# The end of the first block of a fused retention and Mish kernel: the next block's attention output one group of products sooner, its scores before the last small product, its sums before the last output addition

## The chip, the cores and the metric

The kernel runs on one core of one Trainium2 chip. The metric is the device time of one execution, in microseconds. Three runs of the kernel before took 198.63, 197.92 and 197.9 us, a median of 197.92 us. The profile is a further execution of its own.

The core's engines work side by side, each through its own list of instructions, and they meet at semaphores: TensorE (PE in the profile, with its weight loads as PEld), VectorE (DVE), ScalarE (ACT), GpSimd (POOL), and SyncE (SP), which here only issues transfers.

## The reference

The inputs are q, k and v of 4 batches, 8 heads, 768 positions and 64 features, and two weight matrices of 512 by 2048 and 2048 by 512. First comes a recurrence with a decay for each head, then a layer with the Mish activation on its 3072 rows:

```
gamma = 1.0 - 2.0 ** (-5.0 - arange(H))
for t in range(S):
    state = gamma * state + einsum('bhd,bhe->bhde', k[:, :, t], v[:, :, t])
    y[:, :, t] = einsum('bhd,bhde->bhe', q[:, :, t], state) / sqrt(D)
x = y.transpose(0, 2, 1, 3).reshape(B * S, H * D)
h = x @ w_in
g = h * tanh(log1p(exp(h)))
out = g @ w_out
```

## The kernel before, in words

The 3072 rows are cut into 24 chunks of 128 positions, six to a batch. In each chunk the recurrence becomes matrix products: scores of keys against queries, a mask (a product with a triangle), scores times values for the present chunk, the state carried from the chunks before times the queries for the past, and an outer product of keys and values for the next state. The chunks are worked in blocks: a first block of four chunks (0 to 3) and then ten blocks of two (4 and 5, 6 and 7, and so on). After the attention output of a block comes its first weight product with Mish, called g1 here, and then its second one, g2.

The blocks of two do both weight products with seven part products in place of eight, over sums and differences of quarters of the operands. Two sets of sums matter here. `x_sums` (lines 639 to 646) makes four sums of quarters of the attention output of a block, four VectorE instructions on lines 643 to 646. Inside `g1_seven`, `snap` copies a part product from PSUM to SBUF on ScalarE (line 677), and `plus` adds it to another part product on VectorE (line 687).

The order of all instructions is written out by hand: each engine does its own in the order in which the functions are called, and a semaphore makes it wait where it needs another engine's work. An engine that waits for one instruction starts nothing that stands behind it. While block n is in its second product, the attention output of block n+1 is made: `scores` (line 438), `mask` (line 444), and `y_two`, which makes the present part (line 507), the outer products (line 453) and the past part (line 489 for the first batch, 498 for others) on TensorE, and then copies the result to SBUF as `xt` on ScalarE (line 540).

The change lies in `first_g2`, the second product of the first block. Its 512 rows are four row groups, written as (p, i) with pair p and i of 0 or 1. Each row group has an output of 512 columns, which is gathered in one PSUM bank: t0[p] for (p, 0), with halves pb and pe, and t1[p] for (p, 1), with halves px and pz. The 2048 features of the hidden layer are in four slices of 512. Slices 0 and 2 go through the seven products, slices 1 and 3 through plain ones. All of first_g2's products but those of slice 3 are on line 1007. Slice 3 comes last, in `end` (line 1065): for each row group two times two matrix products of 512 columns, first half 0 for all four row groups, then half 1 for all four, and behind each half 1 the closing work `ended`: for i = 0 one VectorE addition of 512 columns (line 1071), for i = 1 a VectorE addition of 256 columns (line 1073) and a ScalarE copy of the other 256 (line 1074), which waits for that addition.

Behind first_g2, `x_sums(1)` is called, and then `g1_seven` of block 1 (chunks 4 and 5). Its PSUM tiles take the banks over as they come free: the first product (px) takes the bank of (0, 0), the second (pb) that of (0, 1), the plain product h0 that of (1, 0), and pe that of (1, 1). These are the steps of g1_seven's beginning, in its order:

```
mm(px, a(0, 0), b(0, 0), True)     # 8 matmuls, L670
m1 = snap(px)                      # ACT copy, L677
mm(pb, a(0, 1), b(1, 0), True)     # 8 matmuls, L670
c11 = plus(pb, m1)                 # DVE, L687
h0 = plain(1, 0)                   # 8 matmuls, L694
mm(px, s(2), t(2))                 # 8 matmuls, L670, adds to px
mish_of(0, 0, c11)                 # ACT, L681
u2 = snap(px)                      # ACT copy, L677
mm(pe, s(1), t(1), True)           # 8 matmuls, L670
```

The fifth product adds to the same px that m1 is copied from, so it waits until that copy is done.

Of the kernel before, what the change touches and what calls it, by code (L numbers as in the profile page):

```python
# [16 lines left out]
def kernel(  # L17
# [81 lines left out]
    for c in range(2):  # L99
        t = tri_first[c * HB:(c + 1) * HB]  # L100
# [26 lines left out]
    FIRST = 1  # L127
# [60 lines left out]
    def cast_wout(s, on_act=0):  # L188
        src = wtmps.pop(("out", s))
        t = wouts[s] = cpool.tile([P, FPS, d_model], FP16, name=f"wout{s}")  # L190
        n = FPS - on_act
        if n:
            nc.vector.tensor_copy(t[:, :n], src[:, :n])
        for f in range(n, FPS, 2):
            nc.scalar.copy(t[:, f:f + 2], src[:, f:f + 2])
# [161 lines left out]
    def room16(g):  # L357
        if g not in cast:
            qk16 = castp.tile([P, 2, H, D], FP16, name="qk16")
            cast[g] = (qk16[:, 0], qk16[:, 1], castp.tile([P, H, D], FP16, name="v16"), qk16)  # L360
        return cast[g]
# [6 lines left out]
    def cast_q(g):  # L368
        if g < NCK:
            f = qs.rearrange("p (x j) -> p x j", x=2).unsqueeze(3)  # L370
            nc.gpsimd.tensor_tensor(  # L371
                by_head(g, room16(g)[0]), by_head(0, loaded[g][0]),
                f.broadcast_to((P, 2, HP, D)), op=ALU.mult)

    def bring_k(g):
        if g < NCK:
            b, c = divmod(g, NCH)
            src = k[b, :, c * C:(c + 1) * C].rearrange("h p d -> p h d")
            if g < NCH:
                nc.gpsimd.dma_start(room16(g)[1], src)  # L380
                return
            for x in range(2):
                nc.gpsimd.dma_start(  # L383
                    room16(g)[1][:, x::2], src[:, HP * x:HP * x + HP])

    def cast_v(g):
        if g < NCK:
            nc.gpsimd.tensor_tensor(  # L388
                room16(g)[2], loaded[g][2], vs.unsqueeze(2).broadcast_to((P, H, D)), op=ALU.mult)

    def casts(g):
        cast_q(g)
        cast_v(g)

    def gate(x):
        nc.gpsimd.tensor_copy(gate_t, x)  # L396
# [45 lines left out]
    def mask(g):  # L442
        am = tpp.tile([P, 2, HP, C], FP16, name="am")
        nc.vector.tensor_tensor(  # L444
            am, ats.pop(g), tri.unsqueeze(1).unsqueeze(1).broadcast_to((P, 2, HP, C)),
            op=ALU.mult)
        ams[g] = am
# [127 lines left out]
    def some_late(n):  # L575
        for _ in range(min(n, len(late))):
            late.pop(0)()
# [57 lines left out]
    def x_part(blk, i, j):  # L635
        n = NBP // 2
        return xts[blk][:, i * n:(i + 1) * n, j * P:(j + 1) * P]

    def x_sums(blk):
        t = tsums[blk] = hp.tile([P, 4, NBP // 2, P], FP16, name="xsum", tag="xsum")  # L640
        sub = ALU.subtract
        b = [[x_part(blk, i, j) for j in range(2)] for i in range(2)]
        nc.vector.tensor_tensor(t[:, 0], b[0][1], b[0][0], op=sub)
        nc.vector.tensor_tensor(t[:, 1], b[1][1], t[:, 0], op=sub)
        nc.vector.tensor_tensor(t[:, 2], b[1][1], b[0][1], op=sub)
        nc.vector.tensor_tensor(t[:, 3], b[1][0], t[:, 1], op=sub)
# [320 lines left out]
    def g_sum(n):  # L967
        def part(s, i):
            g = gtiles[0, s // 2][:, s % 2 * FPS:(s % 2 + 1) * FPS]
            return g.rearrange("p f (a i t) -> p f a i t", a=2, i=2)[:, :, :, i]  # L970
        s1, s2, s3, s4 = [
            gsums[0].rearrange("p s (f a) t -> p s f a t", a=2)[:, i] for i in range(4)]
        if n == 1:
            nc.vector.tensor_tensor(s1, part(0, 1), part(2, 1), op=ALU.add)
        elif n == 2:
            nc.vector.tensor_tensor(s2, s1, part(0, 0), op=ALU.subtract)
        elif n == 3:
            nc.vector.tensor_tensor(s3, part(0, 0), part(0, 1), op=ALU.subtract)
        else:
            nc.vector.tensor_tensor(s4, part(2, 0), s2, op=ALU.subtract)  # L980

    def first_g2():
        hf = d_model // 2
        pairs = range(CPB // 2)
        t1 = [mmps.tile([P, 2, hf], FP32, name="o_ps", tag="mm") for _ in pairs]
        t0 = [mmps.tile([P, 2, hf], FP32, name="o_ps", tag="mm") for _ in pairs]
        osb = [[op.tile([P, 2, hf], FP32, name="osb", tag="osb") for _ in range(2)] for _ in pairs]
        m5 = [op.tile([P, hf], FP32, name="snap", tag="snap", bufs=3) for _ in pairs]
        pb, pe = [t[:, 0] for t in t0], [t[:, 1] for t in t0]
        px, pz = [t[:, 0] for t in t1], [t[:, 1] for t in t1]  # L990
        sums = gsums[0].rearrange("p s (f a) t -> p s f (a t)", a=2)

        def a(p, i, s):
            return lambda f: gts[0, s * FPS + f][:, (2 * p + i) * P:(2 * p + i + 1) * P]

        def sm(p, i):
            return lambda f: sums[:, i - 1, f, p * P:(p + 1) * P]

        def b(s, j):
            return lambda f: wouts[s][:, f, j * hf:(j + 1) * hf]  # L1000

        def t(i):
            return lambda f: tmats[(i - 1) // 2][:, (i - 1) % 2, f]

        def mm(o_ps, x, w, first=False, last=False):
            for f in range(FPS):
                nc.tensor.matmul(  # L1007
                    o_ps, x(f), w(f), start=first and f == 0, stop=last and f == FPS - 1,
                    skip_group_check=True)

        for p in pairs:
            mm(px[p], a(p, 0, 0), b(0, 0), True)
            nc.scalar.copy(osb[p][0][:, 0], px[p])
        for p in pairs:
            mm(pe[p], sm(p, 1), t(1), True)
            nc.scalar.copy(m5[p], pe[p])
        cast_wout(2, 2)
        some_late(1)
        gate(tmats[0][:, 1, 0, :1])
        casts(CPB)  # L1020
        cast_q(CPB + 1)
        some_late(1)
        g_sum(4)
        some_late(1)
        for p in pairs:
            mm(pz[p], a(p, 1, 1), b(1, 1))
        for p in pairs:
            mm(pb[p], a(p, 0, 1), b(1, 0))
        for p in pairs:
            mm(pb[p], a(p, 0, 2), b(2, 0))  # L1030
        for p in pairs:
            mm(pe[p], a(p, 0, 1), b(1, 1))
        for p in pairs:
            mm(px[p], sm(p, 2), t(2))
            nc.scalar.copy(osb[p][0][:, 1], px[p])
        turn(CPB, True)
        for p in pairs:
            mm(px[p], sm(p, 3), t(3))
            nc.vector.tensor_tensor(osb[p][1][:, 1], px[p], m5[p], op=ALU.add)
        bring_k(CPB + 2)  # L1040
        bring_k(CPB + 3)
        cast_v(CPB + 1)
        for p in pairs:
            mm(pe[p], sm(p, 4), b(2, 1))
        some_late(1)
        outer_fifth(CPB)
        turn(CPB + 1)
        decay_of_first(CPB, nc.vector)
        cast_wout(3, FPS)
        for p in pairs:  # L1050
            mm(px[p], a(p, 1, 1), b(1, 0))
        for p in pairs:
            mm(px[p], a(p, 1, 2), t(4))
        scores(CPB)
        scores(CPB + 1)
        mask(CPB)
        mask(CPB + 1)
        cast_v(CPB + 2)
        cast_q(CPB + 2)
        turn_by_dma(CPB + 2)  # L1060
        load_q(CPB + 4)

        def end(p, i, half):
            for f in range(2 * half, 2 * half + 2):
                nc.tensor.matmul(  # L1065
                    (t0, t1)[i][p], a(p, i, 3)(f), wouts[3][:, f], start=False,
                    stop=f == FPS - 1, skip_group_check=True)

        def ended(p, i):
            if i == 0:  # L1070
                nc.vector.tensor_tensor(osb[p][0], t0[p], osb[p][0], op=ALU.add)
            else:
                nc.vector.tensor_tensor(osb[p][1][:, 1], pz[p], osb[p][1][:, 1], op=ALU.add)
                nc.scalar.copy(osb[p][1][:, 0], px[p])
            row0 = (2 * p + i) * P
            stores.append((1, out[row0:row0 + P], osb[p][i].rearrange("p j c -> p (j c)")))

        ends = [(p, i) for p in pairs for i in range(2)]
        for p, i in ends:
            end(p, i, 0)  # L1080
        for p, i in ends:
            if (p, i) == (1, 0):
                y_two(1)
            end(p, i, 1)
            ended(p, i)

    def turn_and_load(g):
# [61 lines left out]
        }  # L1149

    first_block()
    x_sums(FIRST)
    gsums.append(gp.tile([P, 4, NFB // 2, P], FP16, name="gsum", tag="g0"))
    for blk in range(FIRST, len(BLOCKS)):
        steps = steps_of_first(blk) if blk == FIRST else steps_of(blk)
# [33 lines left out]
```

## Time and profile before

| | us |
|---|---|
| three runs | 198.63, 197.92, 197.9 |
| median | 197.92 |
| the profiled execution's own time | 198.56 |
| its span | 196.8 |
| PE busy | 189.7 |
| PEld busy | 157.9 |
| DVE busy | 141.8 |
| ACT busy | 105.4 |
| POOL busy | 93.1 |

The span runs from the first to the last instruction of the profiled execution; 1.76 us of its time lie outside. Times in the views below are microseconds from the start of the span. In a timeline a row gives the start, the time from the start of the first of the merged instructions to the end of the last, the engine, the line, the operation, the tiles written and read, the shape, and how many instructions were merged; brackets give idle time before it and what ended that. An instruction that needs nothing else starts before its forerunner on the engine has fully ended, so the distance from start to start is often shorter than the duration. The granted clock of TensorE is 1.00 in every stretch.

The change bears on about 42 to 55 us of the span: the end of the first block's second product and the beginning of block 1.

### The profile page before, as it was taken

The page shows a single profiled execution, that of the slowest core. Times are in us where ns is not written, and L with a number is a line of the kernel's source. Part 1 is how long each engine was busy: PE and PEld are TensorE (multiplying, and loading weights), DVE is VectorE, ACT ScalarE, POOL GpSimd, SP SyncE. Part 2 cuts the span into 40 slices and gives each one's busy share as a digit, 9 for nine tenths or more (in the row PEclk, how much of TensorE's full clock was granted, in tenths as well). Part 3 has the DMA queues.
Part 4 walks back from the last instruction along what each step waited for, and adds up shares of the span by engine and source line. Part 5 has one row for each costly group of instructions (what it writes and reads, how often), then busy time and mean ns, then how long its engine had stood idle before and what let it go on. Part 6 is the DMA issues. An engine that isn't in the chain of part 4 may idle for free.

```text
span 196.8 us, 5964 instructions
## 1 busy us (share of the span) xinstructions
PE 189.7 (96%) x2482; PEld 157.9 (80%) x2482; DVE 141.8 (72%) x304; ACT 105.4 (54%) x193; POOL 93.1 (47%) x130
## 2 busy tenths in 40 slices
PE   6999999999999999999999999999999999999992
PEld 2357546875988988988988988988988988988991
DVE  3788699777997596597497596597497596596462
ACT  3464768442853753753754753753843843843930
POOL 4180214694758829818616728728526633110000
PEclk9999999999999999999999999999999999999999
DMA  5999999996799999994989995996988933101102
GB/s 170 350 373 404 405 408 237 335 199 45 136 219 238 214 212 219 241 206 109 170 215 106 217 165 111 146 225 119 173 195 129 206 46 110 55 0 74 39 27 80
DMA packets 95802, 36.06 MB, mean 183 GB/s; under 512 B 82592, under 2 KB 89376, under 8 KB 95776
## 3 DMA queue, kind: packets, MB, share of 16 engines
q1 hardware_dynamic: 74544, 33.04, 64.8%
q0 software_dynamic: 21088, 2.62, 21.0%
q8 instruction: 19, 0.31, 0.6%
q14 instruction: 7, 0.06, 0.1%
q10 hardware_dynamic: 144, 0.03, 0.1%
HBM read 27.30 MB, written 6.29 MB: 171 GB/s over the span
## 4 chain that ended last, share of the span: by engine, by line
PE 90%; DVE 2%; DMA 2%; ACT 2%; issue 1%; DVEq 0%
PE o_ps L775 32%; PE h_ps L694 18%; PE h_ps L670 16%; PE h_ps L555 5%; PE o_ps L1007 5%; PE y_ps L507 3%; PE at L438 3%; DMA qfirst<-in_q_dram 2%; PE h_ps L864 2%; PE y_ps L498 1%; PE o_ps L1065 1%; DVE am L290 1%; PE u_ps L453 1%; DVE st L314 1%; DVE qfirst L220 1%
## 5 line engine op out<-in xcount | busy, mean ns | idle before, releaser
L694 PE MATMUL h_ps<-xt,win 128*128 128x256 f16 x320 | 41.6, 273 | 0.0
L687 DVE TENSOR_TENSOR hsum<-h_ps,hsnap 128x512 f32<-128x512 f32 x30 | 19.8, 688 | 21.0 <-PE h_ps L670 19.0
L775 PEld LDWEIGHTS <-gsum 128*128 128x128 f16 x336 | 30.8, 98 | 4.3
L694 PEld LDWEIGHTS <-win 128*128 128x128 f16 x320 | 29.3, 98 | 3.6
L775 PE MATMUL o_ps<-tmat,gsum 128*128 128x256 f16 (+1 forms) x256 | 28.0, 266 | 0.0
L383 POOL DMA_DIRECT2D qk<-in_k_dram x36 | 27.9, 779 | 0.0
L775 PEld LDWEIGHTS <-g 128*128 128x128 f16 x256 | 23.7, 98 | 2.6
L444 DVE TENSOR_TENSOR am<-at,tri 128x1024 f16<-128x1024 f32 x20 | 24.2, 1215 | 1.1 <-PE at L438 1.1
L681 ACT ACTIVATE g<-hsum 128x512 f16<-128x512 f32 x30 | 18.6, 630 | 11.5 <-DVE hsum L687 11.5
L701 ACT ACTIVATE g<-h_ps 128x512 f16<-128x512 f32 x40 | 22.7, 599 | 2.4 <-PE h_ps L694 2.4
L396 POOL COPY gate<-gsum 128x1 f16<-128x1 f16 x12 | 2.6, 213 | 43.8 <-DVE gsum L741 36.8
L388 POOL TENSOR_TENSOR v<-vf,qvs 128x512 f16<-128x512 f32 x20 | 23.0, 1155 | 0.0
L784 ACT COPY snap<-o_ps 128x256 f32<-128x256 f32 (+1 forms) x32 | 11.4, 359 | 21.6 <-PE o_ps L775 21.5
L677 ACT COPY hsnap<-h_ps 128x512 f32<-128x512 f32 x30 | 16.4, 580 | 11.5 <-PE h_ps L670 11.5
L797 DVE TENSOR_TENSOR osb<-o_ps,snap 128x256 f32<-128x256 f32 (+1 forms) x31 | 12.7, 410 | 12.6 <-PE o_ps L775 11.5
L371 POOL TENSOR_TENSOR qk<-qf,qvs 128x512 f16<-128x512 f32 x20 | 21.7, 1086 | 0.0
L670 PEld LDWEIGHTS <-wsum 128*128 128x128 f16 x320 | 19.5, 98 | 0.5
L775 PE MATMUL o_ps<-wout,g 128*128 128x256 f16 (+1 forms) x168 | 19.3, 268 | 0.0
L540 ACT CAST xt<-y_ps 128x1024 f16<-128x1024 f32 x10 | 10.1, 1012 | 14.6 <-PE y_ps L498 14.4
L670 PE MATMUL h_ps<-xsum,wsum 128*128 128x128 f16 x240 | 16.7, 219 | 0.0
L670 PEld LDWEIGHTS <-win 128*128 128x128 f16 x240 | 15.1, 98 | 1.0 <-issue 0.4
L613 DVE TENSOR_TENSOR gsum<-g 128x256 f16<-128x256 f16 (+1 forms) x30 | 9.9, 331 | 3.8 <-ACT g L681 3.6
(126 smaller groups left out, 294.8 us busy)
## 6 DMA issues: line engine op xcount, KB each, us to landing
vf<-in_v_dram SPq DMA_DIRECT2D x24, 256.0 KB, 5.1
out_dram<-osb SPq DMA_DIRECT2D x22, 256.0 KB, 4.7
qf<-in_q_dram SPq DMA_DIRECT2D x20, 256.0 KB, 4.2
wi<-in_moe_w_in_dram SPq DMA_DIRECT2D x3, 1024.0 KB, 9.9
wt<-in_moe_w_out_dram SPq DMA_DIRECT2D x3, 1024.0 KB, 8.8
qk<-in_k_dram POOLq DMA_DIRECT2D x36, 64.0 KB, 4.0
qfirst<-in_q_dram SPq DMA_DIRECT2D x2, 512.0 KB, 5.0
kf<-in_k_dram SPq DMA_DIRECT2D x4, 256.0 KB, 5.3
```

The source lines that it names most:

```text
L371: nc.gpsimd.tensor_tensor(by_head(g, room16(g)[0]), by_head(0, loaded[g][0]), f.broadcast_to((P, 2, HP, D)), op=ALU.mult)
L383: nc.gpsimd.dma_start(room16(g)[1][:, x::2], src[:, HP * x:HP * x + HP])
L388: nc.gpsimd.tensor_tensor(room16(g)[2], loaded[g][2], vs.unsqueeze(2).broadcast_to((P, H, D)), op=ALU.mult)
L444: nc.vector.tensor_tensor(am, ats.pop(g), tri.unsqueeze(1).unsqueeze(1).broadcast_to((P, 2, HP, C)), op=ALU.mult)
L670: nc.tensor.matmul(h_ps[:, f], w(f, d), x(d), start=first and f == 0 and d == 0, stop=d == n - 1, skip_group_check=True)
L677: nc.scalar.copy(x, h_ps)
L681: nc.scalar.activation(gt[:, 2 * i * FPS:(2 * i + 1) * FPS, j * P:(j + 1) * P], h, AF.Mish, scale=inv_boost3)
L687: nc.vector.tensor_tensor(h, h_ps, x, op=ALU.add)
L694: nc.tensor.matmul(h_ps[:, j], win(s, 2 * half + j, bp), xt(blk, bp), start=bp == 0, stop=bp == NBP - 1)
L701: nc.scalar.activation(gt[:, fb:fb + 2], h_ps, AF.Mish, scale=inv_boost3)
L775: nc.tensor.matmul(t, x(f), w(f)[:, c], start=first and f == 0, stop=f == n - 1, skip_group_check=True)
L797: nc.vector.tensor_tensor(dst[:, c], t, plus[:, c], op=ALU.add)
```

## The change

Three pieces of work are moved; none is added or taken away.

First, the scores and masks of chunks 4 and 5 are put ahead of the last small product of the seven (`a(p, 1, 2)` with `t(4)`, eight matmuls on line 1007). Second, `y_two(1)` stands behind the half 1 of one row group, (0, 0), where it stood behind two. Third, `x_sums(1)`, which stood behind everything of first_g2, stands between the half 1 of the last row group (1, 1) and that group's `ended`.

In the order on the engines this means: on TensorE, 16 matmuls of scores change places with eight matmuls of line 1007, and the whole of y_two goes ahead of two matmuls of line 1065. On VectorE the four sums go ahead of the last addition of line 1073. On ScalarE the copy to xt goes ahead of the line 1074 copy of (0, 1), so that both line 1074 copies stand between it and the copy m1. The lists of GpSimd and SyncE stay as they are.

```
         for p in pairs:
             mm(px[p], a(p, 1, 1), b(1, 0))
-        for p in pairs:
-            mm(px[p], a(p, 1, 2), t(4))
         scores(CPB)
         scores(CPB + 1)
         mask(CPB)
         mask(CPB + 1)
+        for p in pairs:
+            mm(px[p], a(p, 1, 2), t(4))
...
         for p, i in ends:
-            if (p, i) == (1, 0):
+            if (p, i) == (0, 1):
                 y_two(1)
             end(p, i, 1)
+            if (p, i) == (1, 1):
+                x_sums(1)
             ended(p, i)
...
     first_block()
-    x_sums(FIRST)
```

More of the change, by code (lines that the diff above doesn't have):

```diff
@@ L1051, in first_g2 @@
             mm(px[p], a(p, 1, 1), b(1, 0))
-        for p in pairs:
-            mm(px[p], a(p, 1, 2), t(4))
         scores(CPB)
@@ L1057, in first_g2 @@
         mask(CPB + 1)
+        for p in pairs:
+            mm(px[p], a(p, 1, 2), t(4))
         cast_v(CPB + 2)
@@ L1081, in first_g2 @@
         for p, i in ends:
-            if (p, i) == (1, 0):
+            if (p, i) == (0, 1):
                 y_two(1)
             end(p, i, 1)
+            if (p, i) == (1, 1):
+                x_sums(1)
             ended(p, i)
@@ L1151 @@
     first_block()
-    x_sums(FIRST)
     gsums.append(gp.tile([P, 4, NFB // 2, P], FP16, name="gsum", tag="g0"))
```

## The prediction

> **What bounds the kernel now.** I read the page first (span, engines, chain), then the timeline of each engine around the place of the change, then the waits and landings of the operands that are wanted sooner.
>
> ```profile
> span 196.8 us, 5964 instructions
> PE 189.7 (96%) x2482; PEld 157.9 (80%) x2482; DVE 141.8 (72%) x304; ACT 105.4 (54%) x193; POOL 93.1 (47%) x130
> PE 90%; DVE 2%; DMA 2%; ACT 2%; issue 1%; DVEq 0%
> ```
>
> TensorE is busy for 96% of the span and carries 90% of the chain. So a change can gain only where TensorE stands still, and each new stop costs its full length unless TensorE would have stopped later anyway. Where it lacks work is told by a table of stretches (length, TensorE's busy time and its instructions, then the other engines):
>
> ```profile
> 0.00:10.00 10.00, 7.65 (x34) 3.16 (x37) 5.29 (x29) 3.69 (x6) 3.10 (x12) 1.00 0.84 261
> 10.00:20.00 10.00, 9.32 (x202) 6.87 (x203) 8.41 (x10) 5.15 (x9) 4.28 (x5) 1.00 1.08 390
> 150.00:196.80 46.80, 42.90 (x585) 38.80 (x582) 29.61 (x69) 23.32 (x47) 8.84 (x13) 1.00 0.32 75
> ```
>
> Of the 7.1 us without TensorE work these three hold 6.93, the last of them behind its last product, at the end of the span. So behind the first block there is no room in which a delay is made good. The chain shows the one stop at the place of the change:
>
> ```profile
> 47.55 1.02 ACT xt L540
> 48.57 0.04 issue
> ```
>
> Block 1 can't begin before the copy xt is done, and TensorE has too little left to do meanwhile. Its timeline:
>
> ```profile
> 41.96 1.04 PE L1007 MATMUL o_ps<-tmat,g 128*128 128x256 f16 x8
> 42.93 0.62 PE L438 MATMUL at<-qkt 64*128 64x128 f16 x16
> 43.48 2.76 PE L1065 MATMUL o_ps<-wout,g 128*128 128x512 f16 x12
> 46.18 0.64 PE L507 MATMUL y_ps<-am,v 128*64 128x128 f16 x16
> 46.65 0.29 PE L453 MATMUL u_ps<-v,qk 128*64 128x64 f16 x8
> 47.44 1.04 PE L1065 MATMUL o_ps<-wout,g 128*128 128x512 f16 x4
> 48.61 1.05 PE L670 MATMUL h_ps<-xt,win 128*128 128x128 f16 x16
> 49.50 1.04 PE L694 MATMUL h_ps<-xt,win 128*128 128x256 f16 x8
> 50.37 1.06 PE L670 MATMUL h_ps<-xsum,wsum 128*128 128x128 f16 x16
> 52.14 0.61 PE L670 MATMUL h_ps<-xsum,wsum 128*128 128x128 f16 x8
> 53.03 1.04 PE L694 MATMUL h_ps<-xt,win 128*128 128x256 f16 x8
> 55.23 1.04 PE L775 MATMUL o_ps<-wout,g 128*128 128x256 f16 x8
> ```
>
> Twelve matmuls of line 1065 take 2.76 us and four take 1.04, so each further one takes 1.72/8 = 0.215. The four from 47.44 would let the next start at 47.44 + 4 x 0.215 = 48.30; it starts at 48.61. The stop is 0.31 us, and that is all this place has to give.
>
> VectorE and ScalarE in the same stretch:
>
> ```profile
> 41.29 0.69 DVE L429 COPY qkt<-t_ps 128x1024 f16<-128x1024 f16 x1
> 43.37 2.36 DVE L444 TENSOR_TENSOR am<-at,tri 128x1024 f16<-128x1024 f32 x2 [1.06 <-PE at L438]
> 48.15 0.69 DVE L1071 TENSOR_TENSOR osb<-o_ps,osb 128x512 f32<-128x512 f32 x1 [1.20 <-PE o_ps L1065]
> 48.76 0.42 DVE L1073 TENSOR_TENSOR osb<-o_ps,osb 128x256 f32<-128x256 f32 x1
> 49.09 0.28 DVE L643 TENSOR_TENSOR xsum<-xt 128x256 f16<-128x256 f16 x1
> 49.41 0.29 DVE L644 TENSOR_TENSOR xsum<-xt,xsum 128x256 f16<-128x256 f16 x1
> 49.62 0.28 DVE L645 TENSOR_TENSOR xsum<-xt 128x256 f16<-128x256 f16 x1
> 49.82 0.28 DVE L646 TENSOR_TENSOR xsum<-xt,xsum 128x256 f16<-128x256 f16 x1
> 50.10 0.69 DVE L687 TENSOR_TENSOR hsum<-h_ps,hsnap 128x512 f32<-128x512 f32 x1
> 52.86 1.29 DVE L687 TENSOR_TENSOR hsum<-h_ps,hsnap 128x512 f32<-128x512 f32 x2 [0.29 <-PE h_ps L670]
> ```
>
> ```profile
> 46.98 0.37 ACT L1074 COPY osb<-o_ps 128x256 f32<-128x256 f32 x1 [5.33 <-DVE osb L1073]
> 47.55 1.01 ACT L540 CAST xt<-y_ps 128x1024 f16<-128x1024 f32 x1 [0.19 <-PE y_ps L489]
> 49.21 0.37 ACT L1074 COPY osb<-o_ps 128x256 f32<-128x256 f32 x1 [0.65 <-DVE osb L1073]
> 49.48 0.59 ACT L677 COPY hsnap<-h_ps 128x512 f32<-128x512 f32 x1
> 50.83 0.63 ACT L681 ACTIVATE g<-hsum 128x512 f16<-128x512 f32 x1 [0.76 <-DVE hsum L687]
> 51.36 1.06 ACT L677 COPY hsnap<-h_ps 128x512 f32<-128x512 f32 x2
> 52.30 1.10 ACT L701 ACTIVATE g<-h_ps 128x512 f16<-128x512 f32 x2
> ```
>
> Here the reader is to follow one chain: the addition at 48.76, the line 1074 copy at 49.21 that waits for it, and behind that copy, on the same engine, the copy m1 (line 677) from 49.48 to 50.07. TensorE's fifth product of block 1, at 50.37, adds to the px that m1 copies, and so can't start earlier than 50.07. That cover is 0.30 us.
>
> **The change part by part.** *Scores ahead of the last small product.* The 16 scores and the eight matmuls of line 1007 change places; they take 0.55 (42.93 to 43.48) and 0.97 us (41.96 to 42.93) in either order, so line 1065 still starts at 43.48. The scores of chunk 5 need the VectorE copy of 41.29, done at 41.98; the eight scores of chunk 4 keep TensorE until 41.96 + 0.27 = 42.23. That wait is hidden; without this cover it would be 0.1 at most. The masks start 0.97 sooner, 42.40, and end at 44.76 instead of 45.73. Nothing on TensorE waited for them, so by itself this gives 0.
>
> *y_two one row group sooner.* It starts two matmuls sooner, 46.18 - 0.43 = 45.75. Its operands must be there: masks at 44.76; the values by GpSimd, the keys by transfer:
>
> ```profile
> 40.43 3.05 POOL L383 DMA_DIRECT2D qk<-in_k_dram x4
> 43.46 2.08 POOL L388 TENSOR_TENSOR v<-vf,qvs 128x512 f16<-128x512 f32 x2
> DMA to landing us min/median/max: 2.9/3.1/3.3
> ```
>
> The second cast of v ends at 45.54, and the outer products that read it start at 46.65 - 0.43 = 46.22. The keys of chunk 6 are the first two of the four transfers; the second is issued about 41.2 and lands at most 3.3 later, 44.5. Both are hidden, by 0.68 and 1.7 us; if a cast were later than that, each us over it would be added whole. y_two then ends at 47.01 for TensorE (47.44 - 0.43), and xt is copied from 47.12 to 48.13. TensorE meanwhile has six matmuls of line 1065, until 47.01 + 1.29 = 48.30, so block 1 can begin at about 48.30 instead of 48.61: gain 0.31. On ScalarE the line 1074 copy of (0, 1) now follows xt, about 48.1 to 48.5; the product that takes over its bank starts at 48.30 + 0.44 = 48.74. Hidden, by 0.2.
>
> *x_sums ahead of the last addition.* The half 1 of (1, 0) and of (1, 1) end on TensorE where they ended before, since the same work stands ahead of them. So the line 1071 addition again starts at 48.15, and at 48.76, where the line 1073 addition stood, x_sums starts (xt has been there since 48.13). Its four pitches are 0.32, 0.21, 0.20 (49.09, 49.41, 49.62, 49.82) and a fourth like the third, 0.20: 0.93 us. The addition now runs from 49.69 to 50.11, the copy of line 1074 from 50.14 to 50.51, and m1, 0.27 behind its start as before, from 50.41 to 51.00. What x_sums itself gives is sooner, its second sum at 49.37 instead of 49.70, but TensorE asks for that only from 50.06 on. Nobody on TensorE waited for the sums.
>
> The fifth product of block 1 would now come at 48.30 + 1.76 = 50.06, the distance from 48.61 to 50.37. Its px is free at 51.00, and with the 0.04 that stood between xt and TensorE it starts at 51.04. Stop: 0.98. Against before: 51.04 - 50.37 = +0.67. The gain at xt is swallowed whole, since the end of this stop is set by VectorE and ScalarE, whatever TensorE did before it.
>
> *What is late next.* c11 (line 687) needs m1: 51.03 instead of 50.10, so everything behind it on ScalarE is 0.93 late while TensorE is 0.67 late; the 0.26 between them must come out of the cover that was there. The copy u2 goes to 52.29 to 52.87 (before 51.36), and the product at 52.14 adds to what it copies: 52.14 + 0.67 = 52.81 becomes 52.91, another 0.10. The copy m5 behind it ends at 53.35, where its product comes at 53.36: 0.03. The Mish of h0 (before 52.30, now 53.23 to 53.81) frees the bank of the product of 53.03, now 53.83: 0.02. Then VectorE's sums for the next products follow TensorE again (the second L687 at 52.86 waited for TensorE already), and by the same reckoning no other product of this stretch has less than 0.2 to spare. Together 0.67 + 0.15 = +0.82.
>
> GpSimd's gate on the last sum opens about 0.3 sooner and brings its casts and SyncE's transposing transfer forward by as much; TensorE uses them one block later. 0, bounded by nothing lost since they only come earlier.
>
> The bounds: 0.67 if the three small stops vanish, about 1.1 if pitches are 0.1 longer in each of the chain's links (x_sums beside a GpSimd cast, the addition, the copy). I take 0.82.
>
> *A rule of the skill at the joint.* The whole sum stands on the copy m1 waiting behind a copy it has nothing to do with. The rows show it kept in order: the line 1074 copy of 46.98 idled the engine for 5.33 us, and nothing behind it ran. The Trainium skill ("TensorE: Matmul & The Clock Gate", section "Architectural detail: the array is 16× 32×32, not 1× 128×128") says that ScalarE and VectorE are strict first in, first out, and only TensorE pulls weight loads ahead. By that rule the sum is +0.82; if ScalarE could take m1 first, it would be -0.31. The trace agrees with the rule as far as the 5.33 us go, though there nothing behind the copy was ready.
>
> **The rivals.** *The stop doesn't come (other side).* If m1 starts by 49.43, so that it is done at 50.02, TensorE never stops and only the gain at xt is left: 198.56 - 0.31 = 198.25 in the profiled execution, 197.61 on the median. For it: px is complete by about 48.9. Against it: the line 1074 copy stands ahead of m1, and its addition stands behind four sums; x_sums would have to take 0 instead of 0.93.
>
> *An operand of y_two is late.* If the cast of v or the masks were late, y_two, both halves of (1, 0) and (1, 1) behind it, and the whole chain to m1 move by the excess; it decides from 0.68 us on for the cast. An excess of 0.3 gives +1.1: 199.0 on the median. Against it: neither GpSimd's list nor its transfers move.
>
> *The delay is partly made good.* Where TensorE waits later for something that is fixed in time, the 0.82 shrinks. With the three small stops gone and 0.2 made good it would be +0.47: 198.4. Against it: the table of stretches above leaves under 0.2 us between 20 and 150.
>
> *The chain spreads.* ScalarE's lateness reaches the next products also (the banks of h1, the sums for g2), for a further 0.2 to 0.5: +1.0 to +1.3, 198.9 to 199.2. For it: ScalarE and VectorE are dense here. Against it: from c22 on they wait for TensorE again.
>
> **How the numbers follow.** The profiled execution took 198.56, 1.76 of it outside the span; with +0.82 it would take 199.38. The three runs have a median of 197.92, 0.64 less, with one at 198.63, so executions differ by 0.7 without any change. On the median: 197.92 + 0.82 = 198.74. Chances: the forecast (198.5 to 198.95) 0.62; spreading 0.15; late operand 0.05; partly made good 0.10; no stop 0.08. The range reaches down past the partly made good case, and up by the spread of runs (0.7) on the forecast: 197.9 to 199.5. The case without a stop is left out.
>
> About 0.5% of the time, 0.99 us, is what a measurement can tell from no change. 198.74 is +0.41%, so the forecast itself stays within it unless the runs fall unluckily (0.3 of its 0.62, about 0.19). With spreading and late operand that gives 0.38 for slower by over 0.5%. No case gains 0.99; 0.04 is left for a cause I don't see. Within 0.5%: 0.58.
>
> **What would show it.** In the profile after: xt's copy near 47.1 and block 1 from about 48.3 (right for y_two); masks from about 42.4; x_sums at 48.76, the last addition of line 1073 at about 49.7, m1 at about 50.4; and on TensorE a stop of about 1.0 us ahead of the fifth product, released by m1's line 677. If the fifth product starts near 50.1, the first rival is right and the prediction wrong. If y_two starts after 45.9, an operand was late. If block 1's second product (55.23 before) starts more than 1 us later, the delay spread.

## The result, and the profile after

The changed kernel took 198.76 us (median of nine runs, 198.69 to 199.49), the kernel before 197.92 (nine runs, 197.85 to 198.63). The ratio is 1.0043, with a 95% interval of 1.0025 to 1.0061: slower by 0.84 us on the medians. The interval leaves out a ratio of 1, though the difference is less than the 0.5% (0.99 us) that the prediction took as the least that can be told. The experiments below have runs of the kernel before of their own beside them, with medians of 198.36 to 198.41 us instead of 197.92.

The two spans, 196.8 and 197.0 us, seem to tell only 0.2 us. In the two profiles the first block reached its slice 3 at different times, for a reason that lies ahead of the change. The chain of waits at the very start says which, first before, then after:

```profile
0.74 4.53 DMA qfirst<-in_q_dram
```

```profile
0.74 3.85 DMA qfirst<-in_q_dram
```

The first load of q took 0.68 us less in the profile after, and everything behind it starts that much sooner: the first matmul of line 1065 at 42.82 instead of 43.48. So all places below are told from that matmul, which the change hardly moves against the work ahead of it: it starts 2.39 us behind the row of line 1007 that stands ahead of the moved scores before (41.09), and 2.41 after (40.41). TensorE after the change:

```profile
41.38 0.62 PE L438 MATMUL at<-qkt 64*128 64x128 f16 x16
41.93 1.05 PE L1007 MATMUL o_ps<-tmat,g 128*128 128x256 f16 x8
42.82 2.32 PE L1065 MATMUL o_ps<-wout,g 128*128 128x512 f16 x10
45.07 0.64 PE L507 MATMUL y_ps<-am,v 128*64 128x128 f16 x16
46.33 1.47 PE L1065 MATMUL o_ps<-wout,g 128*128 128x512 f16 x6
47.63 1.06 PE L670 MATMUL h_ps<-xt,win 128*128 128x128 f16 x16
48.53 1.04 PE L694 MATMUL h_ps<-xt,win 128*128 128x256 f16 x8
50.37 1.05 PE L670 MATMUL h_ps<-xsum,wsum 128*128 128x128 f16 x16 [0.81 <-ACT hsnap L677]
52.23 0.61 PE L670 MATMUL h_ps<-xsum,wsum 128*128 128x128 f16 x8
52.72 0.61 PE L670 MATMUL h_ps<-xt,wsum 128*128 128x128 f16 x8
53.22 1.03 PE L694 MATMUL h_ps<-xt,win 128*128 128x256 f16 x8
55.41 1.04 PE L775 MATMUL o_ps<-wout,g 128*128 128x256 f16 x8
```

| from the first matmul of line 1065 to | before | after | difference |
|---|---|---|---|
| y_two (line 507) | 2.70 | 2.25 | -0.45 |
| block 1's first product | 5.13 | 4.81 | -0.32 |
| its fifth product | 6.89 | 7.55 | +0.66 |
| block 1's second product (line 775) | 11.75 | 12.59 | +0.84 |
| the last row of the end, the last products of line 775 | 148.36 | 149.21 | +0.85 |

The last row goes by the starts of the last products, first before, then after:

```profile
191.84 1.06 PE L775 MATMUL o_ps<-tmat,g 128*128 128x128 f16 x16
```

```profile
192.03 1.06 PE L775 MATMUL o_ps<-tmat,g 128*128 128x128 f16 x16
```

The reader is to see that TensorE does gain 0.32 us where the change aims, loses 0.98 between block 1's first and fifth product, another 0.18 up to line 775, and that nothing happens in the 137 us behind that. The bracket at 50.37 names the releaser: the copy m1. It counts 0.81 from the end that the row ahead of it is given; from start to start the stop is 0.98. The chain to it, on VectorE (with the masks of line 444 ahead of it) and ScalarE:

```profile
41.82 2.36 DVE L444 TENSOR_TENSOR am<-at,tri 128x1024 f16<-128x1024 f32 x2 [0.18 <-PE at L438]
47.47 0.69 DVE L1071 TENSOR_TENSOR osb<-o_ps,osb 128x512 f32<-128x512 f32 x1
48.08 0.28 DVE L643 TENSOR_TENSOR xsum<-xt 128x256 f16<-128x256 f16 x1
48.81 0.28 DVE L646 TENSOR_TENSOR xsum<-xt,xsum 128x256 f16<-128x256 f16 x1
49.01 0.42 DVE L1073 TENSOR_TENSOR osb<-o_ps,osb 128x256 f32<-128x256 f32 x1
50.35 0.69 DVE L687 TENSOR_TENSOR hsum<-h_ps,hsnap 128x512 f32<-128x512 f32 x1 [0.93 <-ACT hsnap L677]
```

```profile
46.44 1.01 ACT L540 CAST xt<-y_ps 128x1024 f16<-128x1024 f32 x1 [4.25 <-PE y_ps L489]
49.46 0.37 ACT L1074 COPY osb<-o_ps 128x256 f32<-128x256 f32 x1 [1.66 <-DVE osb L1073]
49.73 0.59 ACT L677 COPY hsnap<-h_ps 128x512 f32<-128x512 f32 x1
```

Addition at 49.01, copy at 49.46, m1 at 49.73 to 50.32, fifth product at 50.37. ScalarE stood idle for 1.66 us ahead of the copy of line 1074, with m1 behind it.

### The profile page after: what moved, and what is told of

It is laid out like the page before. It is cut to its first block, busy times and chain, and to the rows that moved or that the text cites. A ratio compares the mean times of both kernels' runs of the same rounds, so it can differ in the third digit from the quotient of the medians.

```text
span 197.0 us, 5964 instructions
## 1 busy us (share of the span) xinstructions
PE 189.1 (96%) x2482; PEld 157.9 (80%) x2482; DVE 141.6 (72%) x304; ACT 105.6 (54%) x193; POOL 92.3 (47%) x130
## 4 chain that ended last, share of the span: by engine, by line
PE 89%; DVE 3%; ACT 2%; DMA 2%; issue 1%; DVEq 0%
PE o_ps L775 32%; PE h_ps L694 18%; PE h_ps L670 16%; PE h_ps L555 5%; PE o_ps L1007 5%; PE y_ps L507 3%; PE at L438 3%; DMA qfirst<-in_q_dram 2%; PE h_ps L864 2%; PE y_ps L498 1%; PE o_ps L1065 1%; DVE am L290 1%; PE u_ps L453 1%; DVE st L314 1%; DVE qfirst L220 1%
```

## The experiments

Theory: x_sums makes the last addition late, that makes the copy of line 1074 late, and m1 stands behind that copy in ScalarE's list. Rivals: the move of y_two does it; the scores do; or the late addition holds TensorE in another way than through m1's place. The measure in all runs is the time from the first matmul of line 1065 to the first of line 775, "the stretch" (11.75 before, 12.59 after).

**Each part alone.** The sums alone (run e1_sums_only):

```
         for p, i in ends:
             if (p, i) == (1, 0):
                 y_two(1)
             end(p, i, 1)
+            if (p, i) == (1, 1):
+                x_sums(1)
             ended(p, i)
...
-    x_sums(FIRST)
```

> The kernel before with x_sums alone moved ahead of the last addition. Measure: the time from the start of the first matmul of line 1065 to the start of the first matmul of line 775 (before 11.75 us, after the change 12.59). Theory (the copy m1 stands behind a line 1074 copy, that behind the addition, that behind four sums): the stop ahead of the fifth product of block 1 ends at the same place whether or not y_two moved, so the whole loss is here: 12.57, +0.8 us on the run. Rival (the stop comes of y_two and the xt copy standing ahead of another row group's closing work): 11.75, and no difference in time.

Measured: ratio 1.0031 (1.0020 to 1.0042), median 199.16 against 198.41 us. TensorE's rows of this run (their "x16" at 50.84 begins with the fifth product, the last row is line 775):

```profile
43.28 2.76 PE L1065 MATMUL o_ps<-wout,g 128*128 128x512 f16 x12
48.40 1.05 PE L670 MATMUL h_ps<-xt,win 128*128 128x128 f16 x16
50.84 1.05 PE L670 MATMUL h_ps<-xsum,wsum 128*128 128x128 f16 x16 [0.51 <-ACT hsnap L677]
55.88 1.04 PE L775 MATMUL o_ps<-wout,g 128*128 128x256 f16 x8
```

The stretch is 12.60. Block 1 begins at 5.12, as before, and yet the fifth product comes at 7.56, where it came after the whole change (7.55). So the end of the stop does not depend on whether TensorE begins block 1 at 5.12 or at 4.81, and the whole loss is the sums'.

y_two alone (run e2_y_only):

```
-            if (p, i) == (1, 0):
+            if (p, i) == (0, 1):
                 y_two(1)
```

> The kernel before with y_two alone moved, masks as late as before. Theory: the masks end in time (about 45.7 on the scale of before, y_two from about 45.75), block 1 begins about 0.3 sooner, but the copy m1 still ends where it ended before, so the fifth product is held by about 0.05 and the copies u2 and m5 hold the next products by 0.1 to 0.2: of 0.31 only about 0.1 is left, 11.65, -0.1 us. Rival (nothing behind block 1's beginning is late, the gain is whole): 11.44, -0.3 us. Rival (y_two is what makes the change slow): 12.5.

Measured: ratio 1.0001 (0.9992 to 1.0011), which can't tell 0.1 us from nothing; the stretch can:

```profile
43.71 2.33 PE L1065 MATMUL o_ps<-wout,g 128*128 128x512 f16 x10
48.53 1.06 PE L670 MATMUL h_ps<-xt,win 128*128 128x128 f16 x16
50.34 1.05 PE L670 MATMUL h_ps<-xsum,wsum 128*128 128x128 f16 x16
55.37 1.04 PE L775 MATMUL o_ps<-wout,g 128*128 128x256 f16 x8
```

11.66. Block 1 begins at 4.82, 0.31 sooner, the fifth product at 6.63, 0.26 sooner, line 775 only 0.09 sooner. So two thirds of the gain from y_two are lost even without the sums' move, because ScalarE and VectorE are no sooner: m1 starts 5.98 behind the first matmul of line 1065, before 6.00.

The scores alone (run e3_scores_only):

```
-        for p in pairs:
-            mm(px[p], a(p, 1, 2), t(4))
         scores(CPB)
         scores(CPB + 1)
         mask(CPB)
         mask(CPB + 1)
+        for p in pairs:
+            mm(px[p], a(p, 1, 2), t(4))
```

> The kernel before with the scores and masks alone moved. Theory: 11.75 and no difference in time, since nothing on TensorE waited for the masks; they end about 1 us sooner. Rival (the scores wait for the copy of chunk 5's transposes, or break up the stream of products): up to 0.2 more.

Measured: ratio 1.0002 (0.9992 to 1.0012), the stretch 11.73. This part does nothing that can be measured.

**The place of m1.** Two edits of the changed kernel that leave the sums where they are. In the first (run e4_copy_first), the copy of line 1074 goes ahead of the sums (and so of the addition):

```
             if (p, i) == (1, 1):
+                nc.scalar.copy(osb[p][1][:, 0], px[p])
                 x_sums(1)
             ended(p, i)      # no longer makes this copy for (1, 1)
```

> The changed kernel with one more edit: the line 1074 copy of the last row group (1, 1) stands ahead of the four sums, so that it doesn't wait for the addition behind them; the addition now waits for the copy. The sums stay where the change put them. Theory: the copy m1 runs about 1.4 us sooner than in the changed kernel, the stop of 0.8 is gone, and TensorE keeps the gain at block 1's beginning but for about 0.1 (c11 is still behind four sums): 11.5, -0.2 to -0.25 us against the kernel before. Rival (the sums themselves, or the lateness of the addition, hold TensorE): 12.4 or more, as slow as the changed kernel.

Measured: ratio 0.9992 (0.9984 to 1.0001), the stretch 11.57; no stop ahead of the fifth product, which starts 1.77 behind the first, as before:

```profile
43.26 2.32 PE L1065 MATMUL o_ps<-wout,g 128*128 128x512 f16 x10
48.08 1.06 PE L670 MATMUL h_ps<-xt,win 128*128 128x128 f16 x16
49.85 1.06 PE L670 MATMUL h_ps<-xsum,wsum 128*128 128x128 f16 x16
54.83 1.04 PE L775 MATMUL o_ps<-wout,g 128*128 128x256 f16 x8
```

In the second (run e6_m1_first), the copy stays as late as it is, and only m1 goes ahead of it:

```
         m1 = snap(px)
+        while behind_m1:
+            behind_m1.pop()()      # the copy of (1, 1), put off by ended
         mm(pb, a(0, 1), b(1, 0), True)
```

> The changed kernel with one edit: on ScalarE the copy m1 stands ahead of the line 1074 copy of the last row group (line 1076 here), not behind it. That copy still waits for the addition behind the four sums, and is as late as in the changed kernel. Theory (only m1's place in ScalarE's list makes the stop): m1 runs about 1 us sooner, the stop of 0.8 is gone, 11.57, about -0.2 us against the kernel before. Rival (what holds TensorE is the late addition or the late copy themselves, through the bank of the last row group): 12.4 or more, as slow as the changed kernel.

Measured: ratio 0.9992 (0.9982 to 1.0002), the stretch 11.58. ScalarE and TensorE of this run (line 1076 is the copy, 1067 and 777 are 1065 and 775 of the others):

```profile
49.49 0.59 ACT L677 COPY hsnap<-h_ps 128x512 f32<-128x512 f32 x1 [0.54 <-PE h_ps L670]
50.61 0.37 ACT L1076 COPY osb<-o_ps 128x256 f32<-128x256 f32 x1 [0.54 <-DVE osb L1075]
```

```profile
43.97 2.32 PE L1067 MATMUL o_ps<-wout,g 128*128 128x512 f16 x10
50.55 1.09 PE L670 MATMUL h_ps<-xsum,wsum 128*128 128x128 f16 x16
55.55 1.04 PE L777 MATMUL o_ps<-wout,g 128*128 128x256 f16 x8
```

The copy starts at 6.64, exactly where it starts in the changed kernel (49.46 - 42.82), and the addition is as late too. With m1 at 5.52 instead of 6.91 the fifth product comes at 6.58 and the stop is gone. So m1's place behind the addition and the copy makes the stop; their lateness itself costs TensorE about 0.04 us here (from the fifth product to the second plain product, at 51.48, it takes 0.93 us, in e4_copy_first 0.89). It is hidden by very little: the late copy ends at 50.98, and pe, which takes over the bank that it reads, is due 0.44 us behind the fifth product, at 50.99.

**The rest of the gain.** e4_copy_first and e6_m1_first keep 0.18 and 0.17 of 0.32 us. The four sums still stand ahead of c11, which ScalarE's next work waits for. So the sums were split, two ahead of the last addition and two behind c11 (run e5_split_sums; a second argument of `x_sums` now tells which of the four are made):

```
                 nc.scalar.copy(osb[p][1][:, 0], px[p])
-                x_sums(1)
+                x_sums(1, (0, 1))
...
-            "p2": [(gate_x, blk), (cast_q, a - 1), (bring_k, a), (sum_next, a - 2)],
+            "p2": [(x_sums, blk, (2, 3)), (gate_x, blk), (cast_q, a - 1), (bring_k, a), (sum_next, a - 2)],
```

> The copy ahead of the sums as in e4_copy_first, and of the four sums only the first two ahead of the last addition; the last two follow behind the addition c11 (line 687). Theory: what kept e4_copy_first from the whole gain is that c11, and behind it ScalarE's Mish and the copies u2 and m5, come behind four sums. With c11 about 0.4 sooner, the products behind the fifth are no longer held: from the first matmul of line 1065 to the first of line 775 in 11.45 us (before 11.75, e4_copy_first 11.57), -0.3 us against the kernel before. Rival (those products are held by the pace of ScalarE's own work, whatever c11 does): 11.57, as e4_copy_first.

Neither came: it was slower than before, ratio 1.0016 (1.0004 to 1.0027), with a stretch of 11.63 and 0.49 us lost up to the last product. Up to the product of 53.03 (9.55 before, 9.28 here) it went as the theory says, without a hold. Then VectorE and GpSimd, in their own rows:

```profile
51.34 1.53 DVE L592 TENSOR_TENSOR tmat<-wout,wout 128x1024 f16<-128x1024 f16 x1
54.00 1.57 DVE L593 TENSOR_TENSOR tmat<-wout,tmat 128x1024 f16<-128x1024 f16 x1
```

```profile
50.77 1.56 POOL L371 TENSOR_TENSOR qk<-qf,qvs 128x512 f16<-128x512 f32 x1
53.96 1.06 POOL L388 TENSOR_TENSOR v<-vf,qvs 128x512 f16<-128x512 f32 x1
```

GpSimd's cast of q waits at a gate for the fourth sum. Measured from line 1065, that gate opened 1.00 us later than in e4_copy_first (7.41 against 6.41), and the cast fell on lines 591 and 592 of VectorE, the next cast on line 593. Line 592 took 1.53 us instead of 0.68, and the first cast 1.56 instead of 1.04. The Trainium skill ("SBUF — State Buffer", section "SBUF: two separate sides") says that VectorE instructions with two inputs in SBUF and GpSimd instructions that read SBUF shut each other out of a common port for a whole instruction; the rows 1.53 and 1.56, against 0.68 and 1.04 apart, agree with that. The first cast ended 1.53 us later than in e4_copy_first (9.11 against 7.58 from line 1065), 1.00 of it from the later gate and 0.52 from its own longer time. Behind it the transposing transfer for chunk 7 was late, and the scores that read it waited:

```profile
56.46 0.40 PE L438 MATMUL at<-qkt 64*128 64x128 f16 x8 [0.24 <-DMA qkt<-qk]
```

The sixteen scores take 0.97 us from start to start with this wait, 0.56 in the next run. Another 0.20 goes at line 507 behind them, whose sixteen matmuls take 0.84 instead of 0.64: VectorE's second mask runs from 59.55 to 60.76, and line 507 has begun at 60.38.

To tell the split from the cast's new place, the gate was made to read the second sum instead of the fourth, so that the cast comes before line 591 (run e7_gate_sooner); this takes the later gate and the collision away together:

```
-            "p2": [(x_sums, blk, (2, 3)), (gate_x, blk), (cast_q, a - 1),
+            "p2": [(x_sums, blk, (2, 3)), (gate, tsums[blk][:, 1, 0, :1]), (cast_q, a - 1),
```

> As e5_split_sums, with one operand changed: GpSimd's gate ahead of its cast of q reads the second sum, not the fourth, so that the cast starts about 1.4 us sooner and ends before VectorE comes to lines 591 and 592. Theory (in e5_split_sums the cast ran beside line 592 and both took longer, 1.53 us instead of 0.68 on VectorE and 1.56 instead of 1.04 on GpSimd, and that, with the later transposing transfer behind the cast, ate the gain): line 592 takes 0.68 again, the transfer is in time, and from the first matmul of line 1065 to the first of line 775 it takes 11.45 us (before 11.75, e5_split_sums 11.63), -0.3 us against the kernel before. Rival (the split of the sums itself costs, whatever GpSimd does): 11.63, as slow as e5_split_sums.

Measured: ratio 0.9989 (0.9979 to 1.0000), median 198.19 against 198.36 us, the stretch 11.44, and -0.32 us up to the last product. TensorE no longer stops:

```profile
43.26 2.32 PE L1065 MATMUL o_ps<-wout,g 128*128 128x512 f16 x10
48.08 1.06 PE L670 MATMUL h_ps<-xt,win 128*128 128x128 f16 x16
49.84 1.06 PE L670 MATMUL h_ps<-xsum,wsum 128*128 128x128 f16 x16
54.70 1.04 PE L775 MATMUL o_ps<-wout,g 128*128 128x256 f16 x8
```

```profile
49.40 1.04 POOL L371 TENSOR_TENSOR qk<-qf,qvs 128x512 f16<-128x512 f32 x1
```

```profile
50.01 0.58 DVE L645 TENSOR_TENSOR xsum<-xt 128x256 f16<-128x256 f16 x1
51.65 0.68 DVE L592 TENSOR_TENSOR tmat<-wout,wout 128x1024 f16<-128x1024 f16 x1
```

The cast now falls on the third sum, which takes 0.58 instead of 0.28, where there is time for it, and line 592 takes 0.68 again. What kept e4_copy_first from the whole gain was the late c11, as the theory has it. Measured from line 1065, c11 starts at 6.53 there and at 6.14 here (the two rows below, in this order), the copy u2 at 7.78 and 7.40, and the product behind u2, which was held there and is not here, at 8.40 and 8.35.

```profile
49.79 0.68 DVE L687 TENSOR_TENSOR hsum<-h_ps,hsnap 128x512 f32<-128x512 f32 x1
```

```profile
49.40 0.69 DVE L687 TENSOR_TENSOR hsum<-h_ps,hsnap 128x512 f32<-128x512 f32 x1
```

This version keeps the whole gain of y_two in the trace. On the clock it is ahead of the changed kernel (their intervals against the kernel before don't meet), and ahead of the kernel before by an interval that just reaches 1.0000.

## Why the prediction was right

It was right in its mechanism, in the links of the chain and in the sum, and the experiments bear it out rather than the time alone; one small reading and one argument in it do not hold. By its own steps, in the measure from line 1065:

- *Scores ahead.* Worth 0, as forecast: 11.73 against 11.75 alone. The masks started 0.89 sooner, not 0.97, because the scores did. The forecast gave the eight matmuls of line 1007 a length of 0.97 in either order; behind the scores they take 0.89 from start to start (41.93 to 42.82), and the row that now stands ahead of the scores takes 0.97 (40.41 to 41.38). VectorE follows the first score by 0.44 in both profiles.
- *y_two sooner.* Gain at block 1's beginning 0.32, forecast 0.31. Its operands were there: line 507 came 0.45 sooner, forecast 0.43.
- *x_sums.* The addition at 6.19, the copy at 6.64, m1 at 6.91; the forecast had 6.21, 6.66 and 6.93. The fifth product came 0.66 later, forecast 0.67. That the end of this stop does not depend on what TensorE did before was the boldest step, and e1_sums_only shows it.
- *What is late next.* Three small holds of 0.10, 0.03 and 0.02 were forecast, 0.15 together. The distances from the fifth product on were 1.86, 0.49 and 0.50, before 1.77, 0.45 and 0.44: holds of 0.09, 0.04 and 0.06, of which 0.18 is left at line 775. The sum was +0.84 in the trace and on the medians, forecast +0.82.
- *The rivals.* The stop came, so the rival without one fell; the later blocks made nothing good and added nothing (+0.84 at line 775, +0.85 at the end), so the rivals of a spreading and of a partly made good delay fell; no operand of y_two was late. The table of stretches, which the forecast set against a partly made good delay, is weaker than it says, for it counts only 0.13 of the 0.31 us stop at xt as time without work (47.44 + 1.04 = 48.48, to 48.61). The last two rows of the result's table are what shows that nothing was made good.
- *The rule at the joint.* The forecast said that the 5.33 us of idle time had nothing ready behind them, so didn't prove the order. The 1.66 us after the change nearly do: in e6_m1_first m1 started as soon as px was complete, 0.70 us behind the start of block 1 (49.49, released by line 670, against 48.79); by that px was complete at about 48.33 in the changed kernel, and m1 still came at 49.73, behind the copy. e6_m1_first settles it: put ahead in the list, m1 ran 1.1 us before that copy. In these runs ScalarE kept its list's order. The Trainium skill ("TensorE: Matmul & The Clock Gate", section "Architectural detail: the array is 16× 32×32, not 1× 128×128") says so, and the trace agrees.

One thing the forecast gave a price of 0 in its sum, and only a tenth of a microsecond in its upper bound: where GpSimd's casts fall against VectorE. In the changed kernel that came out well by luck: line 591 took 0.68 instead of 0.92, since the cast came 0.35 sooner and line 591 itself 0.91 later. In e5_split_sums, whose expectation left the casts out, they cost the gain. That the median agrees to 0.02 us is more than the method can do: runs of one kernel differ by 0.7.

## What to carry to other kernels

Work that looks free on an idle engine is not free if it is put ahead of an instruction that something else waits behind: follow the moved instruction to the next engine's list and look what stands behind the waiter there. Here four sums of 0.93 us, which nobody on TensorE needed sooner, took the place of one addition, and the price was paid two engines further on. And before a stop is shortened, find what ends next: with the stop at xt gone, the copies on ScalarE were the limit, and only with c11 sooner as well did the whole 0.32 us arrive.

## What the runs showed of the hardware that was not expected

The first load of q landed 0.68 us apart in the profiles of before and after (4.53 and 3.85 us in the chain), about as much as the runs of one kernel differ (0.7). Whether the other runs differ for that reason was not measured. The load is not all that moves: in e6_m1_first it landed 0.06 us later than in the kernel before, and the first matmul of its line 1067 (1065 before) came 0.49 later. From line 1065 to the last products, the kernel before and e3_scores_only, which differ in nothing that costs time, agree to 0.03 us (148.36 and 148.33). So two spans can hide a change of this size, 0.2 us between the spans and 0.85 in the place itself, and an anchor behind the first loads shows it.

VectorE's sums and differences of 128x1024 fp16 elements, with both inputs in SBUF, took 0.68 us alone, 0.92 where they met only the end of a GpSimd cast, and 1.53 and 1.57 in e5_split_sums; one of the two casts there took 1.56 instead of 1.04, the other 1.06. e5_split_sums and e7_gate_sooner differ in nothing but the operand of GpSimd's gate, and by 0.81 us from line 1065 to the last products (148.85 and 148.04), about as much as the whole change cost.
